# An H3 and squared-ReLU kernel: the last unit's token preparation begins two steps ahead of the unit, with other distances, and weights are advanced ahead of the merges in the steps before it

## The chip, the cores and the metric

The kernel runs on one core of a Trainium2 chip. The metric is the device time of one execution in microseconds (us), the median of several runs. Profiles come from separate, profiled executions of the same program.

## The reference

Two layers are applied twice, in the order H3, MLP, H3, MLP, to 2048 tokens of 1024 features in float32:

```python
def _A_ref(q, k, v, shift_k, ssm_k, ssm_D):       # H3 state-space layer
    k_shift = causal depthwise conv of k with shift_k (4 taps)
    kv = k_shift * v
    y = causal long convolution of kv with ssm_k, over all 2048 tokens (FFT in the reference)
    y = y + kv * ssm_D
    return q * y
def _B_ref(x, w1, b1, w2, b2):                    # MLP, hidden size 3584
    h = x @ w1 + b1
    r = where(h > 0, h, 0)
    return (r * r) @ w2 + b2

x = A_q
x = x + _A_ref(_layernorm(x), A_k, A_v, A_shift_k, A_ssm_k, A_ssm_D)
x = x + _B_ref(_layernorm(x), B_w1, B_b1, B_w2, B_b2)
x = x + _A_ref(_layernorm(x), ...)                # same weights again
x = x + _B_ref(_layernorm(x), ...)
```

## The kernel before

**Units.** The MLPs are worked in units of one layer and one block of 512 tokens: `ORDER = [(0, 0), (1, 0), (0, 1), (0, 2), (1, 1), (0, 3), (1, 2)]`. The sixth of them, layer 0 of block 3, is called the unit ahead here. The last one is the joint unit: layer 1 of blocks 2 and 3 together. `steps` is a list written at build time; a step is the work of one weight tile of 128x1024. TensorE (PE) takes the steps in that order, and every matmul is done three times, with a high and a low half of each factor (`mm3`, lines L353 to L355: high by high, high by low, low by high).

**The unit ahead's end.** It multiplies in seven products of smaller blocks. Its last 28 steps use w2, four steps of six matmuls for each product, and the products come in the order `WORD_END = (0, 3, 5, 6, 4, 2, 1)`. After each product VectorE (DVE) adds the two PSUM banks to running sums (`acc`, `fx`, `fg`; L1691) and merges these sums among themselves (L1696); finished rows go to DRAM by L1702 (`x<-fg`, `x<-acc`). The four token tiles of block 2 for the joint unit are prepared at the same time: load `px` (L861), normalise (ScalarE, ACT, L865), transpose on PE (L874), four copies by ACT (L880 and L881), a store `ed<-px` (L885) and the low half by DVE (L883).

**The joint unit.** It uses seven products over halves of both blocks and of the features, as in Strassen's method. Part a1 has 28 steps of twelve matmuls (numbers 0 to 27), part b1 has 70 (from 28 on), part c2 98. In a1 only block 2's operands are needed. Beside it the four token tiles of block 3 are prepared by `side(st, tt, k)`: k = 0 loads the tile and its H3 result (`px<-x`, `wr<-yd`), 1 takes statistics (DVE, L714 on), 2 combines (L828, L829), 3 takes statistics again and stores the row, 4 makes `nr` (DVE) and normalises (ACT, L1882), 5 transposes (PE, L1890), and 6 to 10 make the operands `tq` (ACT and DVE, L1896 to L1914). `SIDE_AT` gives for each tile the step at which it begins, `SIDE_D` the distance of each k from that step. The first a1 bank of each pair is copied by ACT (L1924), the second is added by DVE (L1938).

**Weights.** A raw weight tile is loaded into a ring of eight rows (`wr`), cast to its high half by ACT (L1102), and its low half `whl<-wr,whl` is subtracted by the engine that `WLO` names for the phase of the step (L1110): V is DVE, G is GpSimd (POOL). Some tiles were split before and come as ready pairs, by one load of 512 KB (L1098, `whl<-wd_m`), which needs no cast. The high and low pairs have a ring of six. From b1 on the weights are sums of four raw tiles `sr`, made by POOL in four instructions (L1063 to L1066) for every two weights. `w_advance` keeps loads, casts and lows a few weights ahead of PE; it can run only as far as the ring's slots are released. Weights of the last product of the unit ahead (j = 1) are ready pairs.

**What sets the order.** Every engine takes its own instructions in the order in which the program wrote them, and all loads and stores named here leave from the queue of SyncE (SP) in its order. A step writes, one after the other, what is due at it (`lag.tick()`: merges, stores, preparation) and the weights (`w_advance`):

```python
phase[0] = "e" if u == NU - 2 and last_step[u] - s < END_G else ...
if phase[0] == "x":
    w_advance(s, top)
    lag.tick()
else:
    lag.tick()
    w_advance(s, top)
```

"x" are steps of single token tiles at the start of a unit. `side`'s calls are entered into `lag` by `make_duo`, which is called at the joint unit's first step. In the last steps of the unit ahead `left` counts the steps to its end.

Of the kernel before, what the change touches and what calls it, by code (L numbers as in the profile page):

```python
# [37 lines left out]
W_LOAD, W_HI, W_LO, W_PAIR = 8, 4, 3, 4  # L38
# [15 lines left out]
WINO = (5,)  # L54
# [10 lines left out]
KEEP_M = 4  # L65
CHAIN = ((2, 3, 3, 7, 8, 8, 9, 13, 13, 14, 14), (2, 3, 3, 7, 8, 8, 9, 12, 12, 13, 13))
NORM = "VAVA"
WLO = {"b": "G", "x": "GGGV", "e": "G", "b1": "VVG", "c2": "VVG"}
SIDE_AT = ((2, 1, 0), (3, 4, 0), (0, 8, 0), (1, 12, 1))
SIDE_D = (0, 3, 4, 5, 6, 9, 10, 11, 12, 13, 14)  # L70
DUO_1 = (3, 6, 7, 5, 4)
DUO_2 = (1, 6, 2, 7, 5, 4, 3)
DUO_W = {1: 0, 2: 1, 3: 2, 4: 3, 5: 4, 6: 5, 7: 6}
DUO_G = 4
END_G = 14
PREP_PACE = 0.2
FWD_RATE = {0: 1.4, 1: 1.4, 2: 1.4, 3: 1.1, 4: 1.1, 5: 1}

# [170 lines left out]
def tile_h3_mlp(ctx: ExitStack, tc: tile.TileContext, q, kT, vT, shk, ssmT, ssmD, w1, b1, w2, b2,  # L249
                fwd_t, pro_t, inv_t, sgn_t, out):  # L250
    nc = tc.nc
    V, A, G, PE, SY = nc.vector, nc.scalar, nc.gpsimd, nc.tensor, nc.sync
# [641 lines left out]
    NU = len(ORDER)  # L894
# [107 lines left out]
    phase = [""]  # L1002
    ptr = {"load": 0, "hi": 0, "lo": 0}
# [14 lines left out]
    def split_kept(key):  # L1018
        k, c, a, i = key
        if k in "st":  # L1020
            return False
        if c == 1:
            return True
        return i == 0 if k == "m1" else (a + i) % 2 == 0

    def from_pair(w):
        return w not in single and split_kept(wsrc[w]) and w - first_w.get(wsrc[w], w) >= PAIR_GAP
# [4 lines left out]
    def room():  # L1032
        return len(ring) < RAWS or ring[-RAWS].get("freed", now[0]) < now[0] - 1
# [34 lines left out]
    def w_load():  # L1068
        w = ptr["load"]
        ptr["load"] += 1  # L1070
        if from_pair(w):
            return
        k, c, a, i = wsrc[w]
        if k == "s":
            if c not in sums:
                sum_load(c)
            if c + 1 < FT // 2 and c + 1 not in asked:
                asked.add(c + 1)
                lag.at(2, sum_ahead, c + 1)
            raws[w] = {"t": sums[c][:, a]}  # L1080
            return
        raws[w] = row()
        raw = raws[w]["t"]
        if k == "t":
            while c not in made:
                next(tgen[0])
            SY.dma_start(raw, TD[c][:, T_AT[a]])
        elif k == "m1":
            SY.dma_start(raw, w1[c * FC + a, :, 4 * i:4 * i + 4])
        else:  # L1090
            f = c * FC + i
            SY.dma_start(raw, w2[f * P:(f + 1) * P, a * 512:(a + 1) * 512])

    def w_hi():
        n = ptr["hi"]
        t = his[n] = mw.tile([P, 2, 512], F32R, name="whl", bufs=6)
        if from_pair(n):
            SY.dma_start(t.bitcast(F32), WD[wsrc[n]])  # L1098
        else:
            if wsrc[n][0] == "s":  # L1100
                sum_make(wsrc[n][1])
            A.copy(t[:, 0], raws[n]["t"])  # L1102
        ptr["hi"] += 1

    def w_lo():
        n = ptr["lo"]
        t = wts[n] = his.pop(n)
        if not from_pair(n):
            e = WLO.get(phase[0], "V")
            ENG[e[n % len(e)]].tensor_sub(t[:, 1], raws[n]["t"], t[:, 0].bitcast(F32))  # L1110
            drop(raws.pop(n))
        ptr["lo"] += 1
# [7 lines left out]
    def w_advance(s, w):  # L1120
        n = len(wsrc)
        now[0] = s

        def free(k):
            if k >= n or k >= 6 and last_use[k - 6] >= s:
                return False
            return not from_pair(k) or k < 6 or last_use[k - 6] < s - 1

        def ahead(k):
            return w + (W_PAIR if k < n and from_pair(k) else W_HI) + (phase[0] == "x")  # L1130

        while ptr["lo"] < ptr["hi"] and ptr["lo"] <= w + W_LO + 2 * (phase[0] == "x"):
            w_lo()
        while free(ptr["hi"]) and ptr["hi"] <= ahead(ptr["hi"]) and ptr["hi"] < ptr["load"]:
            w_hi()
        while ptr["load"] < n and ptr["load"] <= w + W_LOAD and (from_pair(ptr["load"]) or room()):
            w_load()
        while ptr["lo"] <= w:
            if ptr["load"] <= ptr["hi"]:
                w_load()  # L1140
            if ptr["hi"] <= ptr["lo"]:
                w_hi()
            w_lo()
# [427 lines left out]
    lag = slag  # L1571
    xT = first_block()
# [138 lines left out]
    def load_y(b, tts):  # L1711
        ys = [pre.tile([P, D], F32, name="px", bufs=2) for _ in tts]
        for y, tt in zip(ys, tts):
            SY.dma_start(y, YD[b][:, tt])
        return ys
# [118 lines left out]
            dst = X2[b][:, tt] if l == 0 else tokens(out, b, tt)  # L1834
            SY.dma_start(dst, accs[tt])

    def make_duo(xT):
        b1_, b2_ = DUO
        n_p = FT // 2
        xh, xl = xT  # L1840
# [72 lines left out]
                    else:  # L1913
                        V.tensor_sub(lo, v, hi.bitcast(F32))  # L1914

        lag.at(2, open_arena)
        for n, (tt, t0, late) in enumerate(SIDE_AT):
            st = {"bank": pst if n % 2 else ps1}
            for k, d in enumerate(SIDE_D):
                lag.at(t0 + d + late * (k >= 5), side, st, tt, k)  # L1920

        def keep_1(p, o):
            x = st_p[p]["p1"] = row()
# [197 lines left out]
    for sb in range(1, NB):  # L2121
        if WIN[sb] > lo_u:
# [3 lines left out]
            n = sum(last_step[u] + 1 - start_step[u] - 19 * (1 - PREP_PACE) for u in range(lo_u, hi_u))  # L2126
# [7 lines left out]
    nxt = None  # L2134
# [9 lines left out]
    for s, (k, u, c, a, i, tts, w) in enumerate(steps):  # L2144
        if s < 2 * AHEAD_0:
            continue
        l, b = ORDER[u]
        if u != cur_u:
            cur_u = u
            if u:  # L2150
                xT = nxt
            bst = {}
            if u == NU - 1:
                duo = make_duo(xT)
            elif u in WINO:
                wacc, rp = {}, {}
                lag.at(11, load_wacc, wacc, b)
                lag.at(34, load_b2, bst)
                lag.at(38, add_b2w, bst, wacc)
            else:  # L2160
                if not (u and direct[u - 1]):
                    accs = []
                    lag.at(5, load_acc, accs, b)
                lag.at(12, load_b2, bst)
                lag.at(16, add_b2, bst, accs)
        if u == NU - 1:
            phase[0] = k
            lag.tick()
            w_advance(s, w)
            duo(k, c, a, wts[w], xT)  # L2170
            if last_use[w] == s:
                wts.pop(w)
            continue
        phase[0] = "e" if u == NU - 2 and last_step[u] - s < END_G else "" if len(tts) == NT else "x" if k == "m1" else "b" if tts[0] else ""
        top = max(top, w)
        if phase[0] == "x":
            w_advance(s, top)
            lag.tick()
        else:
            lag.tick()  # L2180
            w_advance(s, top)
        wh, wl = wts[w][:, 0], wts[w][:, 1]
        if k == "m1":
# [4 lines left out]
            t0, t1 = tts[0] * P, (tts[-1] + 1) * P  # L2188
# [14 lines left out]
        elif k == "w2":  # L2203
# [6 lines left out]
            hi, lo = rp[i][a]  # L2210
# [13 lines left out]
        else:  # L2224
# [19 lines left out]
            if direct[u] and c == NCH - 1 and a == 0 and i == 0 and tts[0] == 0:  # L2244
# [11 lines left out]
                nxt = (mw.tile([P, KT, T], F32R, name="xh", bufs=1), mw.tile([P, KT, T], F32R, name="xl", bufs=1))  # L2256
# [3 lines left out]
        if last_use[w] == s:  # L2260
            wts.pop(w)
        left = last_step[u] - s
        if direct[u] and left == 40:
            early.append(load_y(b, HALF[0]))
        if u + 1 < NU and not direct[u]:
            n = s - start_step[u]
# [4 lines left out]
            if u in WINO and left == W_PREP:  # L2271
                nxt = prep_w(*ORDER[u + 1], lag)
            elif u not in WINO and left == 18:
# [4 lines left out]
                nxt = prep_b(*ORDER[u + 1], lag)  # L2278
# [13 lines left out]
        while todo > 0:  # L2292
            x = next(pds, 0)
# [62 lines left out]
```

## Time and profile before

| | |
|---|---|
| median of 3 runs | 2680.07 us (2679.81 to 2684.74) |
| the profiled execution | 2686.72 us |
| its span in the trace | 2684.9 us |
| TensorE busy | 2623.7 us, 98% of the span |

The profile lists busy time by engine, the chain of work that ended last, and groups of instructions by source line. The trace behind it gives the start and the duration of each instruction and what ended the idle time before it. All times within the execution are counted from the start of its span. In the trace the unit ahead's last product begins at 2120.50, and part a1 of the joint unit starts at 2132.8 and ends at 2223.63.

### The profile page before, as it was taken

To read this page: it belongs to the slowest core of one execution; us is meant where nothing else is said; L and a number is where in the kernel's file an instruction comes from. 1 tells how busy PE (TensorE), PEld (TensorE's weight loads), DVE (VectorE), ACT (ScalarE), POOL (GpSimd) and SP (SyncE) were. 2 spreads that over 40 slices of the span, in tenths; PEclk is the share of its full clock that TensorE was granted. 3 is DMA by queue.
4 is the path that set the end of the run, shared out by engine and by line. 5 is a ranking of instruction groups with operands and counts; after the bars stand their busy time and mean duration, and the time that the engine had idled before them with its cause. 6 is when DMAs were issued, how large, how long until landed. Compare 5 with 4: busy or idle time off the path is not lost.

```text
span 2684.9 us, 36134 instructions
## 1 busy us (share of the span) xinstructions
PE 2623.7 (98%) x12388; PEld 2197.9 (82%) x12388; DVE 2009.8 (75%) x2948; ACT 1108.6 (41%) x1891; POOL 1027.9 (38%) x651
## 2 busy tenths in 40 slices
PE   7999999899999999999999999999999999999999
PEld 6888787787888888888888888888788778888887
DVE  7879888789887877779677765456777788877553
ACT  4454344443444333343232422345444565454342
POOL 2436665256551744427554275000100207535111
PEclk9999999999999999999999999999999999999999
DMA  8789898689989999888987888689889787888663
GB/s 254 262 300 313 293 305 280 231 292 357 345 296 315 308 329 304 273 300 303 340 303 255 306 293 306 207 260 321 304 296 304 269 323 251 263 247 317 230 194 121
DMA packets 380264, 763.16 MB, mean 284 GB/s; under 512 B 44064, under 2 KB 159408, under 8 KB 377008
## 3 DMA queue, kind: packets, MB, share of 16 engines
q1 hardware_dynamic: 380080, 760.85, 83.3%
q8 instruction: 98, 1.61, 0.2%
q14 instruction: 86, 0.70, 0.1%
HBM read 583.49 MB, written 177.21 MB: 283 GB/s over the span
## 4 chain that ended last, share of the span: by engine, by line
PE 79%; DVE 8%; DMA 8%; issue 2%; ACT 2%; POOL 2%; SPq 1%; DVEq 0%; ACTq 0%; POOLq 0%
PE p L353 22%; PE p L354 22%; PE p L355 22%; PE pt L354 2%; PE pt L353 2%; PE pt L355 2%; DMA wr<-w 2%; PE p L1184 2%; DMA whl<-wd_m 2%; DMA cg<-gd 1%; DVE whl L1110 1%; POOL cp L543 1%; DVE sm L547 1%; DVE st L714 0%; DMA cx<-xd 0%
## 5 line engine op out<-in xcount | busy, mean ns | idle before, releaser
L543 POOL TENSOR_TENSOR cp<-cx,cg 128x384 f32<-128x384 f32 (+5 forms) x288 | 544.6, 1904 | 567.7 <-DVE sm L547 378.2
L353 PE MATMUL p<-xh,whl 128*128 128x512 f32 (+1 forms) x1504 | 579.1, 385 | 10.6 <-ACT wr L1924 5.7
L355 PE MATMUL p<-xh,whl 128*128 128x512 f32 (+1 forms) x1504 | 574.9, 382 | 3.5 <-DVE whl L1110 3.0
L354 PE MATMUL p<-xl,whl 128*128 128x512 f32 (+1 forms) x1504 | 574.6, 382 | 0.1
L1110 DVE TENSOR_TENSOR whl<-wr,whl 128x512 fp32r<-128x512 f32 x486 | 430.1, 896 | 130.9 <-ACT whl L1102 126.0
L1102 ACT CAST whl<-wr 128x512 fp32r<-128x512 f32 x546 | 332.4, 619 | 468.7 <-PE p L355 291.7
L353 PE MATMUL p<-whl,rh 128*128 128x512 f32 x1204 | 475.9, 395 | 7.1 <-DMA whl<-wd_m 5.7
L354 PE MATMUL p<-whl,rh 128*128 128x512 f32 x1204 | 471.1, 391 | 2.6 <-POOL whl L1110 1.7
L355 PE MATMUL p<-whl,rl 128*128 128x512 f32 x1204 | 470.6, 391 | 0.0
L353 PEld LDWEIGHTS p<-xh,whl 128*128 128x128 f32 x1504 | 284.9, 189 | 66.2 <-ACT wr L1924 6.4
L355 PEld LDWEIGHTS p<-xh,whl 128*128 128x128 f32 x1504 | 284.7, 189 | 59.1 <-DVE whl L1110 3.4
L354 PEld LDWEIGHTS p<-xl,whl 128*128 128x128 f32 x1504 | 284.7, 189 | 52.4 <-DVE xl L1497 0.3
L1587 DVE TENSOR_TENSOR rl<-wr,rh 128x512 fp32r<-128x512 f32 x140 | 141.7, 1012 | 178.7 <-ACT rh L1584 178.6
L353 PEld LDWEIGHTS p<-whl,rh 128*128 128x128 f32 x1204 | 227.3, 189 | 55.9 <-DMA whl<-wd_m 4.8
L1110 POOL TENSOR_TENSOR whl<-wr,whl 128x512 fp32r<-128x512 f32 x60 | 87.5, 1461 | 483.9 <-ACT whl L1102 426.4
L354 PEld LDWEIGHTS p<-whl,rh 128*128 128x128 f32 x1204 | 227.2, 189 | 49.8 <-DVE whl L1110 2.5
L355 PEld LDWEIGHTS p<-whl,rl 128*128 128x128 f32 x1204 | 226.9, 188 | 47.8
L547 DVE TENSOR_REDUCE sm<-cp 128x128 f32<-128x384 f32 (+5 forms) x288 | 249.4, 874 | 10.2 <-POOL cp L543 10.2
L1579 ACT ACTIVATE wr<-p,b1t 128x512 f32<-128x512 f32 x138 | 95.3, 690 | 369.8 <-PE p L355 368.9
L1707 DVE TENSOR_TENSOR acc<-p,acc 128x512 f32<-128x512 f32 x152 | 99.8, 686 | 83.6 <-PE p L355 83.6
L693 POOL TENSOR_TENSOR sm<-sm 128x512 f32<-128x512 f32 x48 | 69.1, 1440 | 136.2 <-DVE sm L547 130.3
L355 PE MATMUL p<-whl,tq 128*128 128x512 f32 x276 | 107.4, 389 | 0.0
(376 smaller groups left out, 4264.0 us busy)
## 6 DMA issues: line engine op xcount, KB each, us to landing
whl<-wd_m SPq DMA_DIRECT2D x318, 512.0 KB, 5.5
wr<-w SPq DMA_DIRECT2D x442, 256.0 KB, 5.5
wd_m<-whl SPq DMA_DIRECT2D x70, 512.0 KB, 6.3
wr<-td SPq DMA_DIRECT2D x112, 256.0 KB, 5.1
cx<-xd SPq DMA_DIRECT2D x48, 512.0 KB, 5.8
cg<-gd SPq DMA_DIRECT2D x48, 512.0 KB, 6.8
tq<-hd SPq DMA_DIRECT2D x24, 1024.0 KB, 7.2
gd<-fg SPq DMA_DIRECT2D x72, 256.0 KB, 6.4
```

The source lines that it names most:

```text
L353: PE.matmul(o, lh, rh, start=start, stop=False)
L354: PE.matmul(o, lh, rl, start=False, stop=False)
L355: PE.matmul(o, ll, rh, start=False, stop=stop)
L543: G.tensor_mul(pr.rearrange("p c i -> p i c"), xt[:, 0:j + 1], gt[:, j::-1])
L547: V.tensor_reduce(sm[:, ty, jj], st["pr"], axis=AX.X, op=OP.add)
L693: E.tensor_add(s[:, 1:3], s[:, 1:3], s[:, 0:1].to_broadcast([P, 2, s.shape[2]]))
L1102: A.copy(t[:, 0], raws[n]["t"])
L1110: ENG[e[n % len(e)]].tensor_sub(t[:, 1], raws[n]["t"], t[:, 0].bitcast(F32))
L1184: PE.matmul(o, lh, r, start=start, stop=stop)
L1579: A.activation(r, st["o"], AF.Relu, bias=b1t[:, st["f"]:st["f"] + 1])
L1587: V.tensor_sub(st["lo"], st["r"]["t"], st["hi"].bitcast(F32))
L1707: V.tensor_add(accs[tt][:, d], o, accs[tt][:, d])
```

## The change

Four things change, all near the border between the unit ahead and the joint unit.

1. `make_duo` is called four steps before the unit ahead ends, and `SIDE_AT` is counted from the joint unit's start: tile 2 begins two steps before it (one step after it, before the change), tile 3 at step 3 (4), tiles 0 and 1 as before at 8 and 12. The fourth tile's extra step from k = 5 on goes away.
2. `SIDE_D`: k = 4 (normalising) comes seven steps behind a tile's begin instead of six.
3. Phase "e", the last steps of the unit ahead, covers 20 steps instead of 14. In it the weights are advanced ahead of what is due, and one high and two lows further.
4. `WLO`: in phase "e" the lows go to DVE instead of POOL, in a1 to POOL instead of DVE.

```diff
-WLO = {"b": "G", "x": "GGGV", "e": "G", "b1": "VVG", "c2": "VVG"}
-SIDE_AT = ((2, 1, 0), (3, 4, 0), (0, 8, 0), (1, 12, 1))
-SIDE_D = (0, 3, 4, 5, 6, 9, 10, 11, 12, 13, 14)
+WLO = {"b": "G", "x": "GGGV", "e": "V", "a1": "G", "b1": "VVG", "c2": "VVG"}
+SIDE_AT = ((2, -2), (3, 3), (0, 8), (1, 12))
+SIDE_D = (0, 3, 4, 5, 7, 9, 10, 11, 12, 13, 14)
+SIDE_L = 4
...
-END_G = 14
+END_G = 20
+WFIRST = ("x", "e")
...
         def ahead(k):
-            return w + (W_PAIR if k < n and from_pair(k) else W_HI) + (phase[0] == "x")
+            return w + (W_PAIR if k < n and from_pair(k) else W_HI) + (phase[0] in WFIRST)
 
-        while ptr["lo"] < ptr["hi"] and ptr["lo"] <= w + W_LO + 2 * (phase[0] == "x"):
+        while ptr["lo"] < ptr["hi"] and ptr["lo"] <= w + W_LO + 2 * (phase[0] in WFIRST):
...
-    def make_duo(xT):
+    def make_duo(xT, off):
...
-        lag.at(2, open_arena)
-        for n, (tt, t0, late) in enumerate(SIDE_AT):
+        lag.at(off + 2, open_arena)
+        for n, (tt, t0) in enumerate(SIDE_AT):
             st = {"bank": pst if n % 2 else ps1}
             for k, d in enumerate(SIDE_D):
-                lag.at(t0 + d + late * (k >= 5), side, st, tt, k)
+                lag.at(off + t0 + d, side, st, tt, k)
...
-        if phase[0] == "x":
+        if phase[0] in WFIRST:
             w_advance(s, top)
             lag.tick()
...
+        if u == NU - 2 and left == SIDE_L:
+            duo = make_duo(nxt, left)
```

Line numbers after the change are two higher in the code named here.

What moves on the engines is seen at three places. The first is SP's queue at the end of the unit ahead; `wd_m_3_0_0` to `wd_m_3_0_6` are the four ready pairs of the last product, `x_115` is where the block's rows go, `ed` stores are those of the token tiles of block 2. Before:

```order
L885 DMA ed_144<-px 128x1024
L1702 DMA x_115<-acc 128x512 x2
L1098 DMA whl<-wd_m_3_0_0_4516 128x1024
L1089 DMA wr<-w 128x512
L1098 DMA whl<-wd_m_3_0_2_4543 128x1024
L1089 DMA wr<-w 128x512
L1098 DMA whl<-wd_m_3_0_4_4574 128x1024
L1089 DMA wr<-w 128x512
L1702 DMA x_115<-fg 128x512 x2
L1098 DMA whl<-wd_m_3_0_6_4603 128x1024
```

After the change the same queue reads, a little further on:

```order
L1100 DMA whl<-wd_m_3_0_0_4516 128x1024
L1091 DMA wr<-w 128x512
L887 DMA ed_144<-px 128x1024
L1704 DMA x_115<-acc 128x512 x2
L1100 DMA whl<-wd_m_3_0_2_4543 128x1024
...
L1704 DMA x_115<-fg 128x512 x2
L1091 DMA wr<-w 128x512
L745 DMA px<-x_115 128x1024
L1867 DMA wr<-yd_107 128x512 x2
L1091 DMA wr<-w 128x512
L1704 DMA x_115<-acc 128x512 x4
L1100 DMA whl<-wd_m_0_4_0_1495 128x1024
```

The first pair's load has moved ahead of the last `ed` store and of two row stores, the fourth (not shown) ahead of the `fg` stores, and tile 2's load (`px<-x_115`) ahead of the last four `acc` stores; the next ready pair of the joint unit, that of its step 4, stands behind these four.

The second place is DVE at the border of the units; `p_19991` and `p_19992` are the banks of the last product but one, `p_20041` and `p_20042` (`p_20083` and `p_20084` after the change) those of the last one. Before:

```order
L1696 TENSOR_TENSOR acc<-acc,fx 128x512 x2
L1691 TENSOR_TENSOR acc<-p_19991,acc 128x512
L1691 TENSOR_TENSOR acc<-p_19992,acc 128x512
L1691 TENSOR_TENSOR acc<-p_20041,acc 128x512
L1691 TENSOR_TENSOR acc<-p_20042,acc 128x512
L1110 TENSOR_TENSOR whl<-wr,whl 128x512
L1938 TENSOR_TENSOR wr<-p_20161,wr 128x512
L1110 TENSOR_TENSOR whl<-wr,whl 128x512
L714 BN_STATS st<-px 128x6 x2
```

and after the change:

```order
L1698 TENSOR_TENSOR acc<-acc,fx 128x512 x2
L1112 TENSOR_TENSOR whl<-wr,whl 128x512
L1693 TENSOR_TENSOR acc<-p_19991,acc 128x512
L1693 TENSOR_TENSOR acc<-p_19992,acc 128x512
L1112 TENSOR_TENSOR whl<-wr,whl 128x512 x3
L716 BN_STATS st<-px 128x6 x2
L717 BN_AGGR mv_20128<-st 128x2
L722 TENSOR_SCALAR ve<-mv_20128 128x1
L1693 TENSOR_TENSOR acc<-p_20083,acc 128x512
L1693 TENSOR_TENSOR acc<-p_20084,acc 128x512
```

The statistics of tile 2, with the load that they wait for, have moved ahead of the eviction of the unit's last product. Further up DVE has nineteen instructions between the lows of the product before and the end of `fg<-fg,fx` that the `fg` stores wait for. ACT casts two more weights there ahead of the four copies of the third token tile of block 2.

The third place is POOL from the end of the unit ahead to the start of b1: L1063 to L1066 make one set of sums. Before:

```order
L1110 TENSOR_TENSOR whl<-wr,whl 128x512 x10
L1063 TENSOR_TENSOR sr<-sr 128x512
L1064 TENSOR_TENSOR sr<-sr 128x512
L1065 TENSOR_TENSOR sr<-sr 128x512
L1066 TENSOR_TENSOR sr<-sr 128x512
L1063 TENSOR_TENSOR sr<-sr 128x512
```

and after the change:

```order
L1112 TENSOR_TENSOR whl<-wr,whl 128x512 x7
L1065 TENSOR_TENSOR sr<-sr 128x512
L1066 TENSOR_TENSOR sr<-sr 128x512
L1067 TENSOR_TENSOR sr<-sr 128x512
L1068 TENSOR_TENSOR sr<-sr 128x512
L1112 TENSOR_TENSOR whl<-wr,whl 128x512
L1065 TENSOR_TENSOR sr<-sr 128x512
L1066 TENSOR_TENSOR sr<-sr 128x512
L1067 TENSOR_TENSOR sr<-sr 128x512
L1068 TENSOR_TENSOR sr<-sr 128x512
L1112 TENSOR_TENSOR whl<-wr,whl 128x512
L1112 TENSOR_TENSOR whl<-sr,whl 128x512
```

Before, three whole sets of sums follow one another and the first two lows of b1 stand behind the third; now the ten lows of the unit ahead are gone from POOL, nine lows of a1 are there, two of them between the sums, and the first low of b1 stands behind the second set, ahead of the third.

## Rows read from the trace of the kernel before

**Rows 1.** The profile's page: span, and busy time by engine.

```profile
span 2684.9 us, 36134 instructions
PE 2623.7 (98%) x12388; PEld 2197.9 (82%) x12388; DVE 2009.8 (75%) x2948; ACT 1108.6 (41%) x1891; POOL 1027.9 (38%) x651
```

**Rows 2.** Stretches: length; busy PE, PEld, DVE, ACT, POOL; clock; DMA; GB/s.

```profile
2120.50:2132.80 12.30, 6.57 (x25) 4.38 (x25) 6.87 (x12) 2.49 (x4) 4.43 (x3) 1.00 1.02 354
2165.00:2193.20 28.20, 26.15 (x119) 20.31 (x117) 27.40 (x60) 15.82 (x30) 0.00 (x0) 1.00 0.85 308
2193.20:2209.90 16.70, 12.06 (x45) 9.65 (x45) 11.96 (x23) 12.65 (x22) 0.00 (x0) 0.80 0.77 268
```

**Rows 3.** Timeline of PE: start, duration, instruction, idle time before and its releaser.

```profile
2104.70 1.03 PE L874 MATMUL p<-ident,px 128*128 128x128 f32 x8
...
2123.18 0.47 PE L353 MATMUL p<-whl,rh 128*128 128x512 f32 x1 [2.52 <-DMA whl<-wd_m]
...
2198.04 0.79 PE L353 MATMUL p<-xh,whl 128*128 128x512 f32 x1 [4.64 <-ACT wr L1924]
...
2203.32 1.38 PE L1890 MATMUL pt<-ident,sr 128*128 128x128 f32 x8
...
2220.91 0.39 PE L353 MATMUL p<-xh,whl 128*128 128x512 f32 x1
...
2223.63 0.39 PE L353 MATMUL pt<-tq,whl 128*128 128x512 f32 x1
```

**Rows 4.** Timeline of SP's queue, the instructions that issue loads and stores.

```profile
2118.56 0.57 SPq L1098 DMA_DIRECT2D whl<-wd_m  x1
...
2122.03 1.22 SPq L1702 DMA_DIRECT2D x<-fg  x2
2123.35 0.39 SPq L1098 DMA_DIRECT2D whl<-wd_m  x1
...
2202.69 0.91 SPq L1051 DMA_DIRECT2D sr<-w  x2
```

**Rows 5.** Timeline of ACT.

```profile
2098.82 0.58 ACT L880 CAST xh<-p 128x512 fp32r<-128x512 f32 x1
...
2101.93 0.62 ACT L1102 CAST whl<-wr 128x512 fp32r<-128x512 f32 x1 [0.54 <-DMA wr<-td]
2102.45 1.52 ACT L865 ACTIVATE px<-px,nr,rs 128x512 f32<-128x512 f32 x2
...
2194.72 1.52 ACT L1882 ACTIVATE sr<-px,nr,rs 128x512 f32<-128x512 f32 x2 [4.08 <-DVE nr L1879]
```

**Rows 6.** Timeline of DVE in part a1.

```profile
2149.34 1.28 DVE L714 BATCH_NORM_STATS2 st<-px 128x6 f32<-128x512 f32 x2
...
2162.47 0.69 DVE L1899 TENSOR_TENSOR sr<-sr,p 128x512 f32<-128x512 f32 x1 [3.22 <-ACT sr L1896]
```

**Rows 7.** Timeline of POOL at the end of part a1.

```profile
2210.13 1.29 POOL L1063 TENSOR_TENSOR sr<-sr 128x512 f32<-128x512 f32 x1 [79.41 <-DMA hd<-wr]
...
2215.82 1.75 POOL L1063 TENSOR_TENSOR sr<-sr 128x512 f32<-128x512 f32 x1
```

**Rows 8.** Line L1110, 2080 to 2232: count, shortest/median/longest in ns, first and last start.

```profile
L1110 DVE TENSOR_TENSOR whl<-wr,whl x26: 678/683/1228, 2080.9 to 2228.6; 128x512 fp32r<-128x512 f32 x26
L1110 POOL TENSOR_TENSOR whl<-wr,whl x10: 1262/1556/1899, 2105.1 to 2129.5; 128x512 fp32r<-128x512 f32 x10
```

**Rows 9.** Tile sr, 2195 to 2232, as in rows 8.

```profile
L1914 DVE TENSOR_TENSOR tq<-sr,tq x2: 684/1236/1789, 2199.8 to 2216.3; 128x512 fp32r<-128x512 f32 x2
```

**Rows 10.** DMA issues, 2095 to 2225: count, size of one, median us from issue to landing.

```profile
wr<-w SPq DMA_DIRECT2D x18, 256.0 KB, 5.7
...
px<-x SPq DMA_DIRECT2D x6, 512.0 KB, 7.6
...
x<-acc SPq DMA_DIRECT2D x6, 256.0 KB, 3.4
...
x<-fg SPq DMA_DIRECT2D x2, 256.0 KB, 7.4
```

More of the change, by code (lines that the diff above doesn't have):

```diff
@@ L2152, in tile_h3_mlp @@
             bst = {}
-            if u == NU - 1:
-                duo = make_duo(xT)
-            elif u in WINO:
+            if u in WINO:
                 wacc, rp = {}, {}
@@ L2159, in tile_h3_mlp @@
                 lag.at(38, add_b2w, bst, wacc)
-            else:
+            elif u < NU - 1:
                 if not (u and direct[u - 1]):
```

## The prediction

> **What bounds the kernel now.** I read the page's first part before anything else: TensorE (PE) is busy 2623.7 of 2684.9 us, 98% [rows 1]. Only time in which PE stands still, or runs at a lower granted clock, can come back; an engine that is merely busy counts where PE waits for it. The table of stretches shows where PE stands still near the edit [rows 2]: in the 12.30 us of the unit ahead's last product it is busy 6.57 (5.7 idle), from 2165 to 2193.2 it loses 2.1, from 2193.2 to 2209.9 another 4.6, and there the granted clock averages 0.80. The step at 2198.04 took 5.3 us (2198.04 to 2203.32, twelve matmuls 0.43 apart instead of 0.23, [rows 3]), where a step of part a1 takes 2.72 (2220.91 to 2223.63, [rows 3]): 2.6 more. Together 15.0 us, 0.56% of the span, is the ceiling. 0.2%, about what a measurement of this kernel can tell from no change, is 5.4 us.
>
> Who is waited for comes from the timelines. In the last product PE waits first for a weight load (the row at 2123.18, [rows 3]); that load left SP at 2118.56, and the fourth at 2123.35, behind the two fg stores at 2122.03 [rows 4]. In a1, the 4.64 us before 2198.04 ended with ACT's copy of a bank (L1924, [rows 3]); ACT was held 4.08 us at L1882 by DVE's nr of the last token tile [rows 5], and DVE was busy 27.40 of the 28.2 us before [rows 2]. So two queues decide: SP in the tail of the unit ahead, DVE in a1.
>
> **The change, part by part.** Times are those of the profiled execution (2686.72 us, 6.65 above the median of 2680.07); I work out a difference and put it on the median. For a common end I take the start of step 29, the second of part b1: PE reached step 28 at 2223.63 [rows 3], so step 29 at 2226.35; behind it the tables set the same order and PE had no idle time.
>
> *Weights ahead of the merges.* SP now issues each of the four paired loads ahead of what held it. The first can leave as soon as PE has released its ring slot, some 2115 (four steps of 1.36, half of a step of a1, before 2120.5); it took 4.6 before (2118.56 to 2123.18, [rows 3, 4]) and so lands before PE wants it. By itself this returns the tail's loss: 12.3 us less four steps, 6.9 us at most. But ACT pays. Two more casts now stand ahead of token tile 1's four copies. The copies ran from 2098.82, while the load for the cast at 2101.93 was still under way [rows 5]; now they start behind that cast, at 2102.45, and with two more casts there are six instructions of 0.52 apart (2101.93 to 2102.45) before the next tile's normalising, which was at 2102.45: it starts at 2105.6 and its two halves end at 2106.4 and 2107.1. PE wanted that tile's transposes at 2104.70 [rows 3]: 1.7 late by the first half, 2.4 by the second; I take 2.0. The last tile's load waits for tile 1's store, now 3.6 later, and by the same count its transposes come 1.7 late. With an estimate of 1.0 for the loads behind the last tile store, the tail loses 4.7 instead of 6.9: it ends near 2130.5, a gain of 2.3 (bounds 0 and 6.9).
>
> *Preparation two steps ahead.* Tile 2 needs the fg store, landed. DVE's merges for it stand behind the lows of the next product, whose load leaves at 2105.4, lands after 5.7 [rows 10] and is cast and split by 2112.3; then come the nineteen instructions that the order has there before the last fg<-fg,fx is done, 0.60 apart (two of 0.68 take 1.28, [rows 6, 8]) and so 11.5 us; the store leaves near 2124.0 (2122.03 before, [rows 4]). Its two issues take 1.2 [rows 4], it lands after 7.4, the px load after 7.6 more [rows 10], the statistics take 1.6 (1.28 of it L714, [rows 6]), and only then does DVE evict the last product, because the statistics stand ahead of it: 2141.8 by these medians. x<-acc stores landed in 3.4 [rows 10]; with that and a quick load it is 2136. I take E = 2139.5. Step 2 of a1 needs those banks, so it starts at E, where it was at 2132.8 + 5.4 = 2138.3: the tail's gain is spent. Behind the evictions stand four x stores, two of which may leave between them (an issue takes 0.39 to 0.6, [rows 4]), and then the load of step 4's weight: 1.3 + 5.7 [rows 10], so step 4 starts at E + 7.
>
> *Longer distances and lows on POOL in a1.* Tile 3's load now follows tile 2's store, which waits for DVE: E + 4.4 (an estimate: four large instructions at L714's 0.68 and the small ones ahead of them), plus 7.6 [rows 10], so its statistics start at E + 12 = 2151.5, against 2149.34 [rows 6]. From there to the last nr took 45.4 before (to 2194.7, [rows 5]). Three subsequent lows leave DVE (0.60 each), the wait of 3.22 for ACT [rows 6] should go, two subtractions move ahead (+1.3), and POOL's lows may cost something: 43 (bounds 41.7 and 45). The last nr comes at E + 55 = 2194.5, as before. Before, the first load for the p sums left SP 8.0 behind that nr, at 2202.69 [rows 4], and POOL began 7.4 later, at 2210.13 [rows 7]. ACT now reaches the squares sooner, since the longer distance puts one bank copy ahead of the normalising: 5.6 instead of 8.0, by most of a step of 2.72 (an estimate). POOL begins at T = 2194.5 + 5.6 + 7.4 = 2207.5.
>
> Five lows that were DVE's now stand between POOL's sums. Four sum operations take 5.7 us (2210.13 to 2215.82, [rows 7]); a low takes 1.26 to 1.90, I use 1.4, and 0.68 on DVE [rows 8]. The low of step 29's weight is the twelfth sum and the fourth low behind T: 17.1 + 5.6 = 22.7. PE cannot start step 29 before 2230.2. Without POOL, it would be there sooner: from E + 7, 16 steps of 2.72 and three groups of transposes (0.87 each: the 1.03 of [rows 3], less the end that overlaps the next step) take 46.1, to E + 53.1; the last tile is normalised at E + 55 + 1.5 [rows 5], a wait of 3.4; 9 more steps and a group of transposes take 25.3: E + 81.8 = 2221.3. POOL is the later, by 8.9.
>
> **Sum.** 2230.2 - 2226.35 = +3.9 us. On the median: **2684 us**. The old waits in the tail and before 2198 mostly go; what is late next is POOL, with waits of PE before steps 25, 27 and 29 of some 4, 2 and 3 us.
>
> Collisions bear on this too. DVE's L1914 took 0.68 at best and 1.79 at worst, the latter while POOL's sums ran [rows 9], and DVE's low 0.68 and 1.23 [rows 8]. The Trainium skill, page "SBUF — State Buffer", section "Who interferes with whom", says a DVE instruction with two SBUF inputs and a GpSimd instruction that reads SBUF exclude each other. By that rule every low moved to POOL can cost DVE more than the 0.6 it saves; the spread in these rows agrees.
>
> **The rivals.**
> 1. *It does what it says: faster.* If the sums' loads reach POOL earlier, or its lows wait for nothing, the 8.9 do not bind and step 29 starts at E + 81.8: 5.0 us sooner with E = 2139.5, 8.5 with E = 2136. For it: in the tail PE's wait has a plain cause in SP's order [rows 3, 4]; POOL is idle for 79.41 us before T [rows 7]. Against: from its issue to POOL's start the sums' load already took 7.4, longer than two steps (5.4). It decides if T is before about 2198.6. Time 2671.5 to 2675.
> 2. *Slower.* Waits before steps 25 to 29 add up and the clock falls once, as behind the 4.64 us wait: +2.6. Five lows that fall in DVE's dense stretch each cost 1.1 (1.79 - 0.68) and save 0.6: nr comes +2.5 later instead of 0 or sooner. 3.9 + 2.6 + 2.5 = +9.0: 2689. The place is POOL's queue at the end of a1, and it decides if the tile-2 load lands after 2139. Against it: the tail's four waits of up to 2.5 left the clock at 1.00 [rows 2].
> 3. *No effect.* The 2.3 of the tail and a1's relief of some 5 equal POOL's delay: within 1 us of before, 2680. For it: E + 55 falls on the same microsecond as the old nr.
>
> **How the numbers follow.** My forecast (POOL binding, +1 to +6) 0.43, rival 1 0.27, rival 2 0.20, rival 3 0.10. Faster by over 0.2%: 0.21 of rival 1 and 0.04 of errors elsewhere, 0.25. Slower: all of rival 2 and 0.09 of the forecast, 0.29. Within: 0.46. The range takes most of rivals 1 and 2: 2672 to 2690; the forecast's own is 2681 to 2686.
>
> **What would show it.** Right: no wait for whl<-wd_m above 1.5 us in the last product; a wait before the transposes of tiles 2 and 3 on ACT; a1's step 2 waiting for DVE's eviction; POOL's first low behind a sum late by 2 us or more for PE, and step 29 released by POOL. Wrong: px landing by 2133, or PE at step 25 without a wait. If tile 2's statistics don't hold DVE, E is wrong and with it all that follows.

## The result, and the profile after

| | runs | median us |
|---|---|---|
| before | 17 | 2683.97 (2678.66 to 2689.23) |
| changed | 17 | 2689.64 (2684.00 to 2692.05) |

The ratio is 1.0023, with a 95% interval of 1.0015 to 1.0030: the changed kernel is 6.2 us slower (4.0 to 8.1). The profiled execution took 2690.72 us. On the page the span and the busy time by engine are, where [rows 1] stood before:

```profile
span 2688.9 us, 36140 instructions
PE 2622.4 (98%) x12388; PEld 2194.8 (82%) x12388; DVE 1996.4 (74%) x2946; ACT 1108.4 (41%) x1891; POOL 1024.7 (38%) x653
```

PE's busy time is 1.3 us less and the span 4.0 us more, so PE stands still longer. What it waits for, from 2080 to 2260, is in the view of PE's waits (line that waits, what ended the wait: us in all, times, longest):

```profile
PE p L876 <- ACT px L867: 3.4, 2, 2.5
PE p L357 <- POOL whl L1112: 3.2, 2, 2.3
PE p L355 <- DMA whl<-wd_m: 3.1, 5, 1.6
PE pt L357 <- POOL whl L1112: 2.8, 1, 2.8
PE pt L1892 <- ACT sr L1884: 2.6, 1, 2.6
PE p L1892 <- ACT sr L1884: 0.5, 1, 0.5
PE p L355 <- ACT wr L1926: 0.4, 1, 0.4
```

The two longest groups of this view before were:

```profile
PE p L353 <- DMA whl<-wd_m: 5.7, 4, 2.5
PE p L353 <- ACT wr L1924: 5.7, 2, 4.6
```

The copy's wait is nearly gone, and the pairs' wait is almost halved (1.37 of the 3.1 in the tail, the rest in a1). New are the normalising in the tail (L867) and POOL's lows, 6.0 us; the wait for the normalising of block 3's tiles (L1884) was 0.3 before and is 3.1.

**Laying two executions beside each other.** Work long before the edit ends a few us earlier or later in every execution, so the start of the span is no common mark: in the fourteen profiles of this document the first of the marks below comes between 2083.2 and 2089.7, whatever the kernel, and behind the second all have 420.4 to 420.9 us left. I take two marks that every kernel here has: the first of the four groups of transposes in the unit ahead's end, and the third group of matmuls on a bank named `pt` in b1, which is behind all that the change moves. Before (both marks), and changed:

```profile
2089.28 1.03 PE L874 MATMUL p<-ident,px 128*128 128x128 f32 x8
...
2264.43 0.39 PE L353 MATMUL pt<-tq,whl 128*128 128x512 f32 x1
```

```profile
2086.60 1.04 PE L876 MATMUL p<-ident,px 128*128 128x128 f32 x8
...
2104.67 1.36 PE L876 MATMUL p<-ident,px 128*128 128x128 f32 x8 [2.49 <-ACT px L867]
...
2213.80 0.50 PE L357 MATMUL p<-xh,whl 128*128 128x512 f32 x1 [2.31 <-POOL whl L1112]
...
2220.40 0.50 PE L357 MATMUL p<-xh,whl 128*128 128x512 f32 x1 [0.86 <-POOL whl L1112]
...
2222.80 0.39 PE L355 MATMUL pt<-tq,whl 128*128 128x512 f32 x1
...
2228.90 0.50 PE L357 MATMUL pt<-tq,whl 128*128 128x512 f32 x1 [2.77 <-POOL whl L1112]
...
2268.30 0.39 PE L355 MATMUL pt<-tq,whl 128*128 128x512 f32 x1
```

The stretch between the marks was 2264.43 - 2089.28 = 175.15 us and is 2268.30 - 2086.60 = 181.70 us, 6.55 more, near the 6.2 of the runs. (With a second profile of each kernel, below, the four differences are 6.55 to 8.55.) The changed execution is 2.68 ahead at the first mark; so 2.68 has to be added to its times before they are set beside those of [rows 3 to 8]. Part b1 begins at 2222.80, 136.20 behind the mark, against 134.35: 1.85 of the loss lies ahead of it. The other 4.7 lie between b1's start and the second mark (45.50 against 40.80): the wait of 2.77 in b1's second step, and what follows it.

POOL's own timeline shows where that wait comes from, in place of [rows 7]:

```profile
2206.34 1.30 POOL L1065 TENSOR_TENSOR sr<-sr 128x512 f32<-128x512 f32 x1 [6.50 <-DVE tq L1916]
...
2212.49 1.26 POOL L1112 TENSOR_TENSOR whl<-wr,whl 128x512 fp32r<-128x512 f32 x1
2213.71 1.29 POOL L1065 TENSOR_TENSOR sr<-sr 128x512 f32<-128x512 f32 x1
...
2219.07 1.28 POOL L1112 TENSOR_TENSOR whl<-wr,whl 128x512 fp32r<-128x512 f32 x1
2220.31 1.29 POOL L1112 TENSOR_TENSOR whl<-sr,whl 128x512 fp32r<-128x512 f32 x1
2221.56 1.30 POOL L1065 TENSOR_TENSOR sr<-sr 128x512 f32<-128x512 f32 x1
...
2227.59 3.74 POOL L1112 TENSOR_TENSOR whl<-sr,whl 128x512 fp32r<-128x512 f32 x3
```

POOL works without a pause from 2206.34 on. The lows that end at 2213.75, at 2220.35 and at 2228.86 (2227.59 plus one low of 1.27) are those that PE waits for at 2213.80, 2220.40 and 2228.90. The last of them stands behind twelve sums and three other lows.

### The profile page after: what moved, and what is told of

Read it like the earlier page. It is cut to its first block, busy times and chain, and to the rows that moved or that the text cites. A ratio compares the mean times of both kernels' runs of the same rounds, so it can differ in the third digit from the quotient of the medians.

```text
span 2688.9 us, 36140 instructions
## 1 busy us (share of the span) xinstructions
PE 2622.4 (98%) x12388; PEld 2194.8 (82%) x12388; DVE 1996.4 (74%) x2946; ACT 1108.4 (41%) x1891; POOL 1024.7 (38%) x653
## 4 chain that ended last, share of the span: by engine, by line
PE 78%; DMA 9%; DVE 6%; POOL 2%; issue 2%; SPq 1%; ACT 1%; DVEq 0%; POOLq 0%; ACTq 0%
PE p L355 22%; PE p L356 22%; PE p L357 22%; PE pt L357 2%; PE pt L356 2%; PE pt L355 2%; DMA wr<-w 2%; PE p L1186 2%; DMA cg<-gd 1%; DMA wd_m<-whl 1%; DVE whl L1112 1%; POOL cp L545 1%; DMA fx<-kT 0%; DMA whl<-wd_m 0%; DMA fx<-vT 0%
```

## The experiments

Ten variants between the two kernels ran, and each of the two was profiled a second time. Ratios are against the kernel before, run on the same chip. The stretch is that between the two marks, in one profiled execution; it was worked out from the timelines as above. A1's lows are the twelve that the program writes during a1: nine for a1's own weights and the first three for b1's, which are made from sums. "Late lows" are the last five of them, those between and behind POOL's sums.

| kernel | late lows of a1 | ratio (95%) | us at 2683 | stretch |
|---|---|---|---|---|
| before | DVE | 1 | 0 | 175.15; again 173.90 |
| changed | POOL | 1.0023 (1.0015 to 1.0030) | +6.2 | 181.70; again 182.45 |
| lows on POOL alone | POOL | 1.0034 (1.0021 to 1.0047) | +9.1 | 181.71 |
| changed, tail undone | POOL | 1.0018 (1.0009 to 1.0027) | +4.8 | 180.91 |
| changed, late lows alone on POOL | POOL | 1.0019 (1.0009 to 1.0028) | +5.1 | 179.08 |
| changed, lows on DVE | DVE | 1.0000 (0.9992 to 1.0009) | 0.0 | 171.31 |
| changed, late lows on DVE | DVE | 0.9994 (0.9985 to 1.0002) | -1.6 | 173.35 |
| tail alone | DVE | 1.0004 (0.9995 to 1.0013) | +1.1 | 173.64 |
| preparation alone | DVE | 0.9990 (0.9981 to 0.9999) | -2.7 | 169.41 |
| preparation, early lows on POOL | DVE | 0.9985 (0.9976 to 0.9994) | -4.0 | 169.95 |
| preparation, tail of ten steps | DVE | 0.9982 (0.9973 to 0.9991) | -4.8 | 170.42 |
| the same, early lows on POOL | DVE | 0.9982 (0.9973 to 0.9990) | -4.8 | 170.31 |

The second column decides the sign: with the late lows on POOL each kernel is slower than before, with them on DVE none is, as far as the intervals tell.

**1. a1's lows back on DVE** (a1_dve).

```diff
-WLO = {"b": "G", "x": "GGGV", "e": "V", "a1": "G", "b1": "VVG", "c2": "VVG"}
+WLO = {"b": "G", "x": "GGGV", "e": "V", "b1": "VVG", "c2": "VVG"}
```

> The changed kernel with one part undone: the low halves of part a1 go to DVE again. Theory (POOL's queue in its order is what ends last): the three waits of PE for POOL's lows at the end of a1 (2.31, 0.86 and 2.77 us) and the half-speed matmuls behind the last of them (1.9) go, 7.9 together, and of these some come back as waits for DVE; the kernel is 4 to 8 us faster than the changed one, within 2 us of the one before. Rival (DVE is the bound of a1): nine lows of 0.60 make the last tile's nr late by up to 5 us, PE waits before that tile's transposes as long as it did before the change, and the kernel stays within 2 us of the changed one, 4 us or more above the one before.

The ratio is 1.0000: the change's whole loss is gone, by this edit alone. PE's waits in the same stretch have no POOL in them:

```profile
PE p L355 <- DMA whl<-wd_m: 3.6, 4, 1.2
PE p L1892 <- ACT sr L1884: 2.6, 1, 2.6
PE p L876 <- ACT px L867: 2.3, 2, 1.3
PE p L355 <- ACT wr L1926: 0.4, 1, 0.4
```

The wait for a normalised tile (2.55) is no longer than in the changed kernel (2.58), so the lows on DVE did not make it later, as the rival had it.

**2. The tail undone** (no_wfirst).

```diff
-WLO = {"b": "G", "x": "GGGV", "e": "V", "a1": "G", "b1": "VVG", "c2": "VVG"}
+WLO = {"b": "G", "x": "GGGV", "e": "G", "a1": "G", "b1": "VVG", "c2": "VVG"}
-END_G = 20
-WFIRST = ("x", "e")
+END_G = 14
+WFIRST = ("x",)
```

> The changed kernel with the unit ahead's end undone (weights behind the merges again, phase e of 14 steps with its lows on POOL); preparation two steps ahead and a1's lows on POOL stay. Theory: the waits of PE for POOL at the end of a1 stay, of 5 to 6 us together, and the tail waits for its ready pairs as before (5.7): 3 to 7 us slower than before. Rival (the weights ahead of the merges are what costs, by the 3.4 us that PE waits for two tiles' transposes): the kernel is at 0 to +2 against before.

It is 4.8 us slower than before, with waits for POOL of 2.68, 0.85 and 2.77. The theory's price holds, and the rival's 0 to +2 does not (2.4 to 7.2): the changed tail is not what cost. One part of the theory did not come: the waits for ready pairs were 2.4 and not 5.7, and a wait of 3.10, at the place of the longest of them, is put down to a merge on DVE.

**3. The preparation alone** (side_only): experiment 2's edit, and a1's lows on DVE.

```diff
-WLO = {"b": "G", "x": "GGGV", "e": "G", "a1": "G", "b1": "VVG", "c2": "VVG"}
+WLO = {"b": "G", "x": "GGGV", "e": "G", "b1": "VVG", "c2": "VVG"}
```

> Of the change only the preparation two steps ahead with its longer distances; weights and lows as before. Theory: no wait for POOL at the end of a1; the 4.64 us wait for ACT's copy and the 2.6 us of lower clock behind it go or shrink to 2.6, the tail stays as before: 1 to 6 us faster than before. Rival (the preparation is what costs): 3 us or more slower than before.

It is 2.7 us faster (0.3 to 5.1). The long wait for ACT's copy is replaced by one of 2.5 for a normalised tile, and no wait for POOL is there:

```profile
PE p L355 <- DMA whl<-wd_m: 5.2, 3, 2.6
PE p L1892 <- ACT sr L1884: 2.5, 1, 2.5
```

So moving the preparation is a gain, with an interval just clear of zero, and it was covered by the lows.

**4. The tail alone** (weights_only): SIDE_AT and SIDE_D of before, make_duo's calls at the joint unit's first step, a1's lows on DVE.

```diff
-SIDE_AT = ((2, -2), (3, 3), (0, 8), (1, 12))
-SIDE_D = (0, 3, 4, 5, 7, 9, 10, 11, 12, 13, 14)
-SIDE_L = 4
+SIDE_AT = ((2, 1, 0), (3, 4, 0), (0, 8, 0), (1, 12, 1))
+SIDE_D = (0, 3, 4, 5, 6, 9, 10, 11, 12, 13, 14)
+SIDE_L = 0
```

> Of the change only the unit ahead's end: weights ahead of the merges, 20 steps, lows on DVE; preparation as before and a1's lows on DVE. Theory: the tail loses 5 instead of 7 us (waits for transposes in place of waits for ready pairs) and a1 is as before: 1 to 3 us faster than before. Rival (ACT's two casts ahead of the copies cost more than the loads give): 1 us or more slower than before.

It measured +1.1 (-1.3 to +3.5), so the gain of 1 to 3 that I expected isn't there, and the rival's loss isn't shown either. PE waited for the ready pairs 2.4 instead of 5.7, but 1.9 for the tiles' normalising, which is new, and 4.63 for ACT's copy in a1 as before: the tail gives back most of what it saves (in this profile it is 42.44 us long from the first mark to a1, and 43.54 before). Its two parts, the weights ahead and the lows on DVE, were not run apart.

**5. The lows on POOL alone** (pool_only): the edits of experiments 2 and 4 together, with a1's lows left on POOL.

> Of the change only a1's lows on POOL; weights and preparation as before. Theory (POOL's order alone ends last): POOL's first sum starts within 2 us of where it did before, and the low of step 29's weight is done 22.5 us behind it (twelve sums, four lows), so PE waits for POOL before the third matmul of steps 25, 27 and 29 again: 3 to 7 us slower than before. Rival (the waits for POOL need the moved preparation; alone, the relief of DVE makes the sums early): no wait for POOL above 0.5 us, -2 to +1.

It is 9.1 us slower (5.6 to 12.6, from five runs), more than I expected, and the highest figure of all. POOL's first sum started at 2208.01, 119.0 behind the first mark (2089.00), where it had been 120.85 behind it; the fourth low ended 23.3 us behind that, and PE waited three times for it:

```profile
2215.47 0.50 PE L357 MATMUL p<-xh,whl 128*128 128x512 f32 x1 [1.36 <-POOL whl L1112]
2222.84 0.50 PE L357 MATMUL p<-xh,whl 128*128 128x512 f32 x1 [1.61 <-POOL whl L1112]
2231.35 0.50 PE L357 MATMUL pt<-tq,whl 128*128 128x512 f32 x1 [2.76 <-POOL whl L1112]
```

The sums began 1.9 earlier, not by the 5.7 that PE's three waits add up to; and the waits need no moved preparation. The wait for ACT's copy in a1 is still there (4.12), as before the change.

**6. The late lows back on DVE, the early seven left on POOL** (after_pool7), and **7. the reverse** (after_late5).

```diff
             e = WLO.get(phase[0], "V")
+            if phase[0] == "a1":
+                a1_lows.append(n)
+                e = "G" if len(a1_lows) <= 7 else "V"      # after_pool7
+                e = "V" if len(a1_lows) <= 7 else "G"      # after_late5
```

> The changed kernel with one thing undone: the last five of a1's twelve lows, those that stand between and behind POOL's sums, go to DVE again; the first seven stay on POOL. Theory (the five late lows cost it all): PE's waits for POOL at the end of a1 and the half-speed matmuls behind them go, 5 to 8 us faster than the changed kernel, -2 to +2 against the one before. Rival (the seven early lows cost as well): 2 us or less faster than the changed kernel.

> The other half: the changed kernel with the first seven of a1's lows on DVE and the last five on POOL. Theory: PE waits for POOL before the same three steps, 5 us or more together, and the time is that of the changed kernel within 2 us: 4 to 8 us slower than before. Rival (twelve lows on POOL are needed): no wait for POOL, 0 to +2.

With the late five on DVE the loss is gone (-1.6, -4.0 to +0.5); with them alone on POOL it is there (+5.1). In the second, PE waited for POOL twice, not three times, and the first time longer (the lows' line is L1117 here):

```profile
2211.81 0.79 PE L357 MATMUL p<-xh,whl 128*128 128x512 f32 x1 [4.12 <-POOL whl L1117]
...
2227.14 0.50 PE L357 MATMUL pt<-tq,whl 128*128 128x512 f32 x1 [2.54 <-POOL whl L1117]
```

This pair splits the edit of experiment 1: five instructions of 1.3 us, by their place in POOL's queue, are the loss.

**8. The preparation with the early seven lows on POOL** (side_pool7): experiment 3 with experiment 6's rule.

> Preparation two steps ahead, weights as before, and of a1's lows the first seven on POOL, the rest on DVE, so that no low stands between POOL's sums. Theory: the order of the late lows is what cost, POOL's early lows cost nothing and take 4.2 us off DVE, so the last tile's normalising comes up to 3 us sooner and PE's wait for it (2.48 with the preparation alone) goes with the lower clock behind it: 3 to 8 us faster than before. Rival (any low on POOL costs, since its cast comes late and POOL takes 1.3 instead of 0.68 for it): 0 to 2 us slower than with the preparation alone, -3 to 0 against before.

At -4.0 the time is where the theory had it, but not by its mechanism: PE's wait of 2.60 for the last tile's normalising stayed. The intervals of this kernel and of experiment 3 overlap, so the early lows' worth isn't shown. The 4.2 us that they take off DVE are not a net relief: beside them other DVE instructions take longer, 2.8 us in this profile and 3.6 in the changed kernel's (see "Collisions" below).

**9. The preparation with a tail of ten steps** (side_end10): experiment 1, and

```diff
-END_G = 20
+END_G = 10
```

> Preparation two steps ahead, a1's lows on DVE, and weights ahead of the merges in the last ten steps alone, behind the last token tiles' casts. Theory: PE no longer waits for ACT before the transposes of the block's last two tiles (1.25 and 1.06 us with twenty steps), the ready pairs are on time but for some 1.5 us: 2 to 6 us faster than before. Rival (the casts are not what made the transposes late): waits for ACT at the transposes above 0.8 us stay, -1 to +2.

It is 4.8 us faster than before (2.4 to 7.2), and the waits at the tiles' transposes, 1.25 and 1.06 in experiment 1, are gone from the list of PE's waits:

```profile
PE p L355 <- DMA whl<-wd_m: 5.8, 6, 2.2
PE p L1892 <- ACT sr L1884: 2.5, 1, 2.5
PE p L355 <- ACT wr L1926: 0.5, 1, 0.5
```

So the casts that twenty steps put ahead of the copies made the transposes late. The waits for ready pairs, those in a1 included, are 5.8 instead of 3.6 in all, so that PE's waits add up to as much as in experiment 1, and the stretch is only 0.9 shorter; that the time is better than experiment 1's is shown by the runs, and not by this list. That ten steps are better than none isn't shown: the interval overlaps that of the preparation alone (-2.7), whose tail is 1.6 us longer in its profile (42.73 against 41.11 from the first mark to a1) and whose a1 is 2.6 shorter (85.88 against 88.51).

**10. Both together** (end10_pool7): experiment 9 with the early seven lows on POOL.

> The changed kernel with phase e of ten steps and the last five lows of a1 on DVE: the parts that gained, put together. Theory (the parts add, as far as PE's waits are separate): 4 to 8 us faster than before. Rival (the wait of 2.5 us for the last tiles' normalising, which none of the parts removed, is what is left, and seven lows on POOL don't shorten it): as with ten steps alone, 3.5 to 5.5 us faster than before.

-4.8 again: the rival was right, the early lows add nothing to experiment 9. The wait of 2.58 for the last tile is still there, and I have not found what would remove it.

**11. and 12. Second profiles of the two kernels** (before_again, after_again).

> The kernel before once more, for a second profile. If the lower clock behind the long wait in a1 comes in every execution, the stretch from the first transposes of the unit ahead's end to the fourth group of b1 is as long as in the first profile, within 0.5 us; if it comes in some executions alone, the stretch is 2 to 3 us shorter and holds no matmuls 0.43 apart.

> The changed kernel once more, for a second profile. Theory: PE waits for POOL before the third matmul of steps 25, 27 and 29 again, within 0.5 us of the first profile each; the half-speed matmuls behind the waits may come at others of them. Rival (the waits were of that execution): one of the three is gone.

Before took 173.90 us between the marks, 1.25 less than in the first profile, and neither case that I had named: there was lower clock in it, at three places instead of one. The changed kernel took 182.45; PE waited 2.65 and 2.53 for POOL, and the short one at step 27 was gone, as the rival said. The other two are where they were, and the stretch is no shorter, so the waits are the kernel's, and how they are split belongs to an execution.

## Why the prediction was right or wrong

It forecast 3.9 us slower, 2684 on the 2680.07 of three runs; measured are 6.2 slower. The range held the time, but "within 0.2%" was given as the likeliest case, and a loss with an interval wholly above zero came. The mechanism, POOL's queue in its order, was the right one. What failed was the sum: it put the lower clock behind the wait at nothing, and it had POOL begin 1.5 too early, where larger errors of its terms partly cancel. Below, a time of the changed kernel that is set beside one of the kernel before has the 2.68 added; those called the trace's, spans in brackets and lines of the profile do not have it.

- **POOL's queue: right.** "Twelve sums and four lows behind T" was priced at 22.7; they took 22.5 (2206.34 to 2228.86). The waits were forecast before steps 25, 27 and 29 at 4, 2 and 3; they came there, before the third matmul of each, at 2.31, 0.86 and 2.77. Experiments 1, 5, 6 and 7 show that the five late lows are the cause.
- **POOL's start: 1.5 late, and so near by luck.** T was put at 2207.5 and was 2209.0. The last nr let ACT begin at 2196.3 (2193.60 in the trace), not at 2194.5. Two errors of opposite sign stand behind that. Tile 3's statistics began at 2148.6, 2.9 before the E + 12 of the forecast. From there to the last nr the sum took 43, with bounds 41.7 and 45; it took 47.7, longer than the 45.4 before:

```profile
2145.90 1.29 DVE L716 BATCH_NORM_STATS2 st<-px 128x6 f32<-128x512 f32 x2 [0.31 <-DMA px<-x]
...
2193.60 1.52 ACT L1884 ACTIVATE sr<-px,nr,rs 128x512 f32<-128x512 f32 x2 [2.13 <-DVE nr L1881]
```

  The sum had shortened this term for lows that leave DVE and for a wait that goes. With the lows on DVE the same length is 47.5 (experiment 1) and 47.7 (experiment 3), so the lows' engine is not in it. What the sum left out is in `SIDE_AT` and `SIDE_D`: the last tile's normalising now stands 13 steps behind tile 3's statistics, and 11 before. That this is the reason was not tested.
- **The sum's last difference.** It set the low's end, 2230.2, against the start of step 29, 2226.35. PE needs that low only at the step's third matmul, which came at 2226.80 before, so the sum's own terms give +3.4. Measured there is +4.8: 2231.58 against 2226.80.
- **The failing step: the sum ended at step 29**, with the sentence that behind it PE had no idle time. It had none, but its clock fell behind the wait, which I had put into rival 2 alone; the sum has it at nothing. The stretch of 2.95 us that begins 1.25 behind the wait's end shows it (columns as in [rows 2]):

```profile
2228.90:2230.15 1.25, 1.25 (x5) 1.05 (x6) 0.00 (x0) 0.00 (x0) 1.25 (x2) 1.00 0.20 75
2230.15:2233.10 2.95, 2.95 (x8) 2.28 (x7) 0.00 (x0) 0.55 (x1) 1.18 (x1) 0.50 0.29 61
```

  Granted clock 0.50, that is 1.2 instead of 2.4 GHz: eight matmuls 0.43 instead of 0.23 apart, 1.6 us. With the 4.8 it makes 6.4 of the 6.55. Of the five profiles with the late lows on POOL, four show six to eight such matmuls behind this wait, and one (experiment 7) none.
- **The tail: waits right, gain too high.** Forecast were 2.0 and 1.7 for two tiles' transposes and 1.0 for loads, 4.7 in all; measured 2.49, 0.92 and 1.37, 4.78. But the unit's end came only 0.65 earlier by the marks (42.89 against 43.54), not 2.3. I had set bare waits after against lost time before: a wait costs 0.16 more than its length between two starts, one before a matmul some 0.1 again behind it, and the first delayed group of transposes took 1.36 instead of 1.03 (the second took 1.36 before as well), so that 4.78 of waits are 6.3 of time, against 6.9. ACT's order in the trace is the one forecast, casts behind copies and the normalising pushed from 2102.45 to 2106.45, where [rows 5] stood:

```profile
2100.82 0.58 ACT L882 CAST xh<-p 128x512 fp32r<-128x512 f32 x1
...
2102.74 1.17 ACT L1104 CAST whl<-wr 128x512 fp32r<-128x512 f32 x2
2103.77 1.54 ACT L867 ACTIVATE px<-px,nr,rs 128x512 f32<-128x512 f32 x2
```

- **E: in its bounds, 2 us early, and it hardly bound.** DVE did hold the last eviction behind tile 2's statistics, which waited for the load:

```profile
2133.14 1.29 DVE L716 BATCH_NORM_STATS2 st<-px 128x6 f32<-128x512 f32 x2 [3.08 <-DMA px<-x]
...
2134.78 1.28 DVE L1693 TENSOR_TENSOR acc<-p,acc 128x512 f32<-128x512 f32 x2
```

  2134.78 is 2137.5 on the old scale, where 2139.5 was taken. The load landed 3.8 us behind its issue (2129.29 in the trace); I had used the median of 7.6. PE waited 0.44 there, and step 2 began at 2138.2, as before (2138.3). The profile puts that wait down to ACT's copy of a bank (L1926, 2134.91 to 2135.48 in the trace), which stood behind the same statistics in ACT's queue; DVE's first eviction ended at the same time (2135.46 in the trace), so it isn't shown which of the two PE needed. The load behind the four x stores was late by 1.57, as forecast in kind.
- **The last tile:** a wait of 3.4 was forecast for its normalising; it was 2.58.
- **Rival 1's price was wrong.** It said 5.0 to 8.5 faster if POOL's lows did not bind. Experiments 1 and 6 take exactly that away and give 0.0 and -1.6. What is in the place of the gain: the waits for the tail's transposes (experiment 9, without them, is at -4.8), and the 2.5 for a normalised tile with the clock behind it. By the marks, experiment 1 was 3.2 us shorter than the mean of the two profiles of before, though its runs tell no difference: a single stretch is good to some 3 us.
- **Collisions: the rule is right, the price of 2.5 is not.** The prediction said that lows on POOL can cost DVE more than they save, and rival 2 took 2.5 us for it. DVE's subtractions on tile `sr`, from which it took the price, were not longer (0.68 each), because no low ran beside them. Other DVE instructions with two SBUF inputs were. In a1 of the changed kernel DVE's small L732 took 1.03 beside a low of POOL, and ended with it, just ahead of the last nr; before, as L730 without POOL beside it, it took 0.22:

```profile
2191.60 1.38 POOL L1112 TENSOR_TENSOR whl<-wr,whl 128x512 fp32r<-128x512 f32 x1 [6.89 <-ACT whl L1104]
2191.96 1.03 DVE L732 SCALAR_TENSOR_TENSOR rt<-rs,ve 128x1 f32<-128x1 f32 x1
```

```profile
2193.89 0.22 DVE L730 SCALAR_TENSOR_TENSOR rt<-rs,ve 128x1 f32<-128x1 f32 x1
```

  Four of the seven early lows held a DVE instruction so, by 0.73 to 1.03 each, 3.6 us together, of the 4.2 that they save DVE; the second profile of the changed kernel has the same four. With a1's lows on DVE (experiments 1 and 3) none of these instructions is long. So the seven lows relieve DVE by 0.6 us in all, where rival 2 had lows on POOL load it by 2.5. In the unit ahead's end the change works the other way: the same pair of merges took 3.48 us beside POOL's lows before, and 1.28 with the lows on DVE:

```profile
2113.70 4.84 POOL L1110 TENSOR_TENSOR whl<-wr,whl 128x512 fp32r<-128x512 f32 x3 [0.26 <-ACT whl L1102]
2113.91 3.48 DVE L1696 TENSOR_TENSOR fg<-fg,fk 128x512 f32<-128x512 f32 x2
```

```profile
2116.61 1.28 DVE L1698 TENSOR_TENSOR fg<-fg,fk 128x512 f32<-128x512 f32 x2
```

  These rows agree with the exclusion that the Trainium skill states (page "SBUF — State Buffer", section "Who interferes with whom"). Rival 2 came true by its lower clock alone, at 1.6 instead of 2.6.

## What to carry to other kernels

Before moving instructions to an idle engine, lay out its queue in order where it next becomes busy: POOL had been idle for most of a1, and the seven lows in that time changed the kernel's time by nothing that could be measured, while five more between and behind the sums cost 5 to 9 us. Price what runs beside them too: the seven held DVE for nearly as long as they relieved it. Price an engine's backlog at its last consumer, and add what PE loses behind a wait: here a wait of 2 to 5 us could bring up to another 2.4 at half the clock. And undo a bundled change part by part: one part of this one was worth 2.7 us, a second was better in ten steps than in twenty (though not shown to be better than left out), and the third hid the first.

## What was not expected of the hardware

Behind a wait of PE the granted clock falls at some places and not at others, in the same kernel. In the first profile of before, the wait of 2.52 in the tail was followed by matmuls 0.23 apart; in the second, the wait of 2.82 at the same place was followed by eight matmuls at half the clock:

```profile
2119.80:2122.50 2.70, 2.70 (x7) 2.02 (x7) 2.70 (x5) 0.67 (x2) 1.25 (x1) 0.50 1.00 391
```

In the first profile of the changed kernel the waits of 2.58 and 2.77 were followed by seven and eight slow matmuls, those of 2.49 and 2.31 by none; with the late lows alone on POOL, the wait of 4.12 by seven and that of 2.54 by none; in the second profile of the changed kernel even a wait of 1.86, for a ready pair, was followed by seven. Most such times cost 1.4 us (seven matmuls, 0.2 each) to 2.4 (twelve, in the first profile of before); after some waits only four or five matmuls are slow. What decides between the places stays open.
